# Decode attention with a gated MLP on one core: the last group of the output projection in four column tiles, as two parts in two banks

## The chip, the core and the metric

The kernel runs on one core of one Trainium2 chip. The metric is the device time of one execution in microseconds (us). Times of a kernel are medians of its executions. A profile is one further look at a single execution, and its span is some 2 us shorter than the time that the run reports.

Two short terms are used throughout. A **landing** is the moment at which the sixteenth of the sixteen DMA engines reports its share of a transfer; the trace keeps a record of each. The **tail** is the time from the last landing of the last group of `wo` (the very last load of the kernel) to the start of the final sum on VectorE.

## The reference

One decode step for 4 sequences: attention over a cache of 4096 keys for 32 heads of 128, its output projected by `wo`, plus a gated MLP, plus the residual. Only the projection matters here.

```python
o = jnp.einsum('bhqk,bhkd->bhqd', p, v_cache)
a = o.transpose(0, 2, 1, 3).reshape(B, Sq, H * Dh) @ wo      # [4, 4096] @ [4096, 640]
return x + a + mlp
```

## The kernel before

The heads are worked on in four groups of eight. For each group the attention output is transposed into `oT`, 128 rows by 8 columns `c` of 4 sequences, and `wo` for the group lies in SBUF as 128 rows by 8 columns `c` by 640. Each `c` needs two matmuls, one for each half (`hf`) of the 640 outputs, so a group takes 16 matmuls of 320 columns with only 4 rows of output each. A column tile is here one of four places for a matmul, told by the partition at which its output starts: 0, 32, 64 or 96. In the trace of this kernel, four matmuls with four different ones start within 10 ns (656.971 to 656.981 us), and the next four 0.22 to 0.27 us later.

The first three groups, the MLP and the residual are summed in one PSUM tile `proj`. They use all four column tiles: even `c` on partitions 0 and 32, odd `c` on 64 and 96.

```python
def emit_proj(g, cs=range(HG)):
    oT = state[("oT", g)]
    for c in cs:
        for hf in range(NH):
            r0 = 64 * (c % 2) + 32 * hf
            nc.tensor.matmul(proj[r0:r0 + B, 0:NO2], lhsT=oT[:, c, :],
                             rhs=wo_t[g][:, c, hf * NO2:(hf + 1) * NO2], start=False, ...)
```

The last group has an accumulator of its own, so that `proj` can be emptied meanwhile, and uses two column tiles only. Its weights come last of all loads, in four pieces.

```python
load_wo(NG - 1, (0, 4, 6, 7, 8))        # c 0..3, 4..5, 6, 7
# ... (cut)
o_1 = ppool.tile([64, NO2], F32, tag="p", name="o_1")
nc.vector.tensor_copy(out=o_1[:], in_=proj[0:64, 0:NO2])                                          # L530
nc.vector.tensor_tensor(out=o_1[:], in0=proj[64:128, 0:NO2], in1=o_1[:], op=ALU.add)              # L531
last = ps_l.tile([64, NO2], F32)
for c in range(HG):
    lhsT = oT[:].rearrange("p c b -> p (c b)") if c == 0 else oT[:, c, :]
    for hf in range(NH):
        nc.tensor.matmul(last[32 * hf:32 * hf + (32 if c == 0 else B), :], lhsT=lhsT,             # L538
                         rhs=wo_t[NG - 1][:, c, hf * NO2:(hf + 1) * NO2], start=(c == 0), stop=(c == HG - 1))
nc.vector.tensor_tensor(out=o_bf[:], in0=last[:], in1=o_1[:], op=ALU.add)                         # L542
nc.sync.dma_start(out=out_flat[:, 0:NO2], in_=o_bf[0:B, :])
nc.scalar.dma_start(out=out_flat[:, NO2:NOUT], in_=o_bf[32:32 + B, :])
```

The first matmul of a half is 32 columns wide so that all 32 rows which VectorE reads later hold something written.

## Time and profile before

| | before |
|---|---|
| time, median of the first 3 runs | 665.66 us (665.23 to 665.97) |
| span of the profiled run | 663.9 us |
| busy share of PE, VectorE, ScalarE | 45%, 54%, 12% |
| read from HBM | 282.25 MB, 425 GB/s over the span |
| last landing | 660.03 us |
| tail | 0.87 us |
| last landing to the end of the span | 3.84 us |

The page gives one busy share for each engine, but these are averages over 660 us, in which no engine is the bound and the transfers are. What the change can move is the last 5 us, and those must be read by themselves. The prediction does so, and shows the lines. One more line is useful beside them: the instructions of the last projection by line of code, with the shortest, median and longest duration in ns and the first and last start.

```profile
L538 PE MATMUL last<-kv,oT x16: 425/471/474, 658.5 to 660.3; 128*4 128x320 bf16 x14, 128*32 128x320 bf16 x2
```

The sixteen matmuls start from 658.5 to 660.3 in 8 rounds of two, and each is in flight 0.47 us: they overlap, so a duration is not what a round costs. The step from one round to the next is.

### The profile page before, as it was taken

The page shows a single profiled execution, that of the slowest core. Times are in us where ns is not written, and L with a number is a line of the kernel's source. Part 1 is how long each engine was busy: PE and PEld are TensorE (multiplying, and loading weights), DVE is VectorE, ACT ScalarE, POOL GpSimd, SP SyncE. Part 2 cuts the span into 40 slices and gives each one's busy share as a digit, 9 for nine tenths or more (in the row PEclk, how much of TensorE's full clock was granted, in tenths as well). Part 3 has the DMA queues.
Part 4 walks back from the last instruction along what each step waited for, and adds up shares of the span by engine and source line. Part 5 has one row for each costly group of instructions (what it writes and reads, how often), then busy time and mean ns, then how long its engine had stood idle before and what let it go on. Part 6 is the DMA issues. An engine that isn't in the chain of part 4 may idle for free.

```text
span 663.9 us, 5636 instructions
## 1 busy us (share of the span) xinstructions
PE 298.9 (45%) x2394; PEld 112.8 (17%) x2394; DVE 360.7 (54%) x331; ACT 77.8 (12%) x162; POOL 10.2 (2%) x35
## 2 busy tenths in 40 slices
PE   0624765266072556225446175542506254633245
PEld 0401211122021122101112022110202112211012
DVE  5248999656190849509164286745628084950002
ACT  0300000430100000530200000070100000062200
POOL 3000000000000000000000000000000000000000
PEclk9998778768576587677757676766958768777767
DMA  9999999999999999999999999999999999999995
GB/s 372 461 434 416 423 451 434 430 435 435 415 442 435 430 414 440 440 430 431 438 438 431 426 422 436 440 438 435 426 430 427 434 433 420 452 431 428 425 414 229
DMA packets 6901, 282.61 MB, mean 426 GB/s; under 512 B 808, under 2 KB 1084, under 8 KB 1468
## 3 DMA queue, kind: packets, MB, share of 16 engines
q1 hardware_dynamic: 6856, 282.25, 98.6%
q8 instruction: 18, 0.29, 0.2%
q14 instruction: 7, 0.06, 0.0%
q10 hardware_dynamic: 20, 0.01, 0.0%
HBM read 282.25 MB, written 0.01 MB: 425 GB/s over the span
## 4 chain that ended last, share of the span: by engine, by line
DMA 71%; issue 12%; DVE 12%; PE 3%; ACT 1%; DVEq 0%; SPq 0%; ACTq 0%
DMA kv<-in_A_k_cache_dram 61%; DVE kT L361 11%; DMA kv<-in_A_v_cache_dram 5%; DMA kv<-in_A_wo_dram 3%; DMA kv<-in_A_wq_dram 2%; PE O L443 2%; PE q L262 1%; PE S L372 0%; ACT xd L426 0%; ACT Zb L407 0%; PE last L538 0%; ACT p L415 0%; DVE pT L419 0%; DVE kv L271 0%; DVE m L379 0%
## 5 line engine op out<-in xcount | busy, mean ns | idle before, releaser
L361 DVE STREAM_TRANSPOSE kT<-kv 128x2048 f32<-128x2048 f32 x128 | 282.8, 2275 | 127.4 <-DMA kv<-in_A_k_cache_dram 125.7
L372 PE MATMUL S<-kT,QZ 128*32 128x512 bf16 x1024 | 190.2, 505 | 232.5 <-DVE kT L361 232.5
L372 PEld LDWEIGHTS <-QZ 128*32 128x32 bf16 x1024 | 61.0, 112 | 356.5 <-issue 337.6
L443 PE MATMUL O<-kv,Zb 128*32 128x512 bf16 x1024 | 75.9, 462 | 59.8 <-DMA kv<-in_A_v_cache_dram 32.8
L450 DVE TENSOR_SCALAR R<-O,Mk 128x128 f32<-128x128 f32 x16 | 5.6, 350 | 126.9 <-PE O L443 126.9
L407 ACT ACTIVATE Zb<-xd,MkE 32x256 bf16<-32x256 bf16 x116 | 52.9, 498 | 109.2 <-PE O L443 107.7
L415 ACT ACTIVATE p<-S,negmax 128x512 bf16<-128x512 f32 x8 | 5.4, 682 | 402.0 <-DVE negmax L393 402.0
L443 PEld LDWEIGHTS <-Zb 128*32 128x32 bf16 x1024 | 33.3, 114 | 101.7 <-issue 60.9
L460 PE MATMUL misc<-R,SelR 128*32 128x128 f32 x32 | 6.4, 281 | 26.0 <-DVE R L452 26.0
L452 DVE SCALAR_TENSOR_TENSOR R<-O,Mk,R 128x128 f32<-128x128 f32 x48 | 16.8, 351 | 1.7
L426 DVE COPY xd<-pT 32x256 bf16<-32x256 bf16 x44 | 16.1, 365 | 0.7
L426 ACT COPY xd<-pT 32x256 bf16<-32x256 bf16 x20 | 12.2, 612 | 5.6 <-DVE pT L419 5.2
L347 POOL COPY QZ<-qT 32x32 bf16<-32x32 bf16 x16 | 5.1, 317 | 418.6 <-PE S L372 400.2
L419 DVE STREAM_TRANSPOSE pT<-p 128x1024 bf16<-128x1024 bf16 x4 | 5.0, 1245 | 6.6 <-ACT p L415 6.6
L460 PEld LDWEIGHTS misc<-R,SelR 128*32 128x32 f32 x32 | 2.2, 107 | 33.5 <-DVE R L452 24.8
L379 DVE TENSOR_REDUCE m<-S 128x2 f32<-128x1024 f32 x4 | 4.9, 1224 | 5.5 <-PE S L372 5.5
L286 PE MATMUL misc<-xnT,kv 128*32 128x4 bf16 (+1 forms) x120 | 6.2, 188 | 0.7 <-DMA kv<-in_B_w_in_dram 0.7
L286 PEld LDWEIGHTS <-kv 128*32 128x32 bf16 (+1 forms) x120 | 6.1, 142 | 1.6 <-DMA kv<-in_B_w_in_dram 1.6
L431 PE MATMUL misc<-rowsum,SelPe 128*32 128x1 f32 x16 | 2.0, 197 | 9.3 <-ACT p L415 9.3
L262 PE MATMUL q<-kv,xnT 128*32 128x512 bf16 x40 | 4.5, 631 | 3.9 <-DMA kv<-in_A_wq_dram 3.9
L463 DVE SCALAR_TENSOR_TENSOR om<-misc,rinv,MkH 32x1024 bf16<-32x1024 f32 x4 | 5.1, 1271 | 2.0 <-PE misc L460 2.0
L384 PE MATMUL misc<-dg,ones_f 128*128 128x256 f32 x8 | 2.7, 416 | 7.5 <-DVE dg L381 7.5
(96 smaller groups left out, 63.6 us busy)
## 6 DMA issues: line engine op xcount, KB each, us to landing
kv<-in_A_k_cache_dram SPq DMA_DIRECT2D x8, 4096.0 KB
kv<-in_A_v_cache_dram SPq DMA_DIRECT2D x1, 6144.0 KB
kv<-in_A_wq_dram SPq DMA_DIRECT2D x1, 5120.0 KB
kv<-in_A_wo_dram SPq DMA_DIRECT2D x3, 1280.0 KB
kv<-in_B_w_in_dram SPq DMA_DIRECT2D x1, 2160.0 KB, 19.8
kv<-in_A_v_cache_dram SPq DMA_DIRECT2D x1, 2048.0 KB
kv<-in_B_w_out_dram SPq DMA_DIRECT2D x1, 800.0 KB
kv<-in_A_wo_dram SPq DMA_DIRECT2D x1, 640.0 KB, 22.5
```

The source lines that it names most:

```text
L262: nc.tensor.matmul(q4_ps[32 * j:32 * j + 32, hf * 512:hf * 512 + 512], lhsT=xnT[:, c, :], rhs=wq[:, c, n0:n0 + 512], start=(c == 0), stop= ...
L286: nc.tensor.matmul(zT_ps[:n, part, fc, :], lhsT=w, rhs=xnT[:, c, 0:B], start=(c == 0), stop=(c == DC - 1))
L347: nc.gpsimd.tensor_copy(out=QZ[r0:r0 + 32, :, :, :, 8 + 8 * hp], in_=qT[32 * g:32 * g + 32, NE * hp:NE * hp + NE].rearrange("p e a b -> p ...
L361: nc.vector.transpose(kT[:].rearrange("p (t r) -> p t r", r=32), kw)
L372: nc.tensor.matmul(S_ps[32 * q:32 * q + 32, e], lhsT=QZ[:, b, 2 * kh + w, e, w0:w0 + 32], rhs=kb[:, i, :, e, :, w], start=(b == 0 and k < ...
L407: nc.scalar.activation(out=dst, in_=src, func=ACT.Copy, scale=mk)
L415: nc.scalar.activation(out=p_bf[:, :, e, :], in_=S_ps[:, e], func=ACT.Exp, bias=negmax[:, e:e + 1], scale=scale, accum_out=rowsum[:, e:e + 1])
L426: op(out=xd[32 * hp:32 * hp + 32, :, q, :], in_=pT[32 * q:32 * q + 32, :, hp, :].rearrange("p t x -> p x t"))
L443: nc.tensor.matmul(O_ps[32 * q:32 * q + 32, :, :], lhsT=Zb[b % 2][:, w].rearrange("p h c -> p (h c)"), rhs=vv[:, w * 4 * Dh:(w + 1) * 4 * ...
L450: nc.vector.tensor_scalar(out=R, in0=O_ps[:, 0, :], scalar1=Mk4[:, 0:1], scalar2=None, op0=ALU.mult)
L452: nc.vector.scalar_tensor_tensor(out=R, in0=O_ps[:, c, :], scalar=Mk4[:, c:c + 1], in1=R, op0=ALU.mult, op1=ALU.add)
L460: nc.tensor.matmul(oh[:], lhsT=SelR[:, b].rearrange("p h b -> p (h b)"), rhs=state["R"][:, b, :], start=(b == 0), stop=(b == B - 1))
```

## The change

Its intent is to project the last group as fast as the groups before it, with four column tiles. Columns 1, 3 and 5 go to partitions 64 and 96 of a second PSUM bank, while 0, 2, 4, 6 and 7 stay in the first. The second part is complete after `c = 5` and is added to `o_1` while PE still works on 6 and 7; then one sum closes as before. The first matmul of the second part reads 32 columns of `oT` from column 1 on, so `oT` has a ninth column of zeros.

```diff
-        oT = small.tile([P, HG, B], BF16, tag="oT", bufs=3)
-        nc.vector.tensor_copy(out=oT[:], in_=oT_ps[:])
+        oT = small.tile([P, HG + 1, B], BF16, tag="oT", bufs=3)
+        nc.vector.tensor_copy(out=oT[:, 0:HG, :], in_=oT_ps[:])
+        if g == NG - 1:
+            nc.gpsimd.memset(oT[:, HG, :], 0.0)
...
-    last = ps_l.tile([64, NO2], F32)
+    last_a = ps_l.tile([64, NO2], F32)
+    last_b = misc_ps([P, NO2], F32)
+    last = [last_a, last_b[64:128]]
     oT = state[("oT", NG - 1)]
+    part = {1: 1, 3: 1, 5: 1}
+    seen = set()
     for c in range(HG):
-        lhsT = oT[:].rearrange("p c b -> p (c b)") if c == 0 else oT[:, c, :]
+        p = part.get(c, 0)
+        lhsT = oT[:, c, :] if p in seen else oT[:, c:c + HG, :].rearrange("p c b -> p (c b)")
+        nb = B if p in seen else 32
         for hf in range(NH):
-            nc.tensor.matmul(last[32 * hf:32 * hf + (32 if c == 0 else B), :], lhsT=lhsT,
-                             rhs=wo_t[NG - 1][:, c, hf * NO2:(hf + 1) * NO2], start=(c == 0), stop=(c == HG - 1))
+            nc.tensor.matmul(last[p][32 * hf:32 * hf + nb, :], lhsT=lhsT,
+                             rhs=wo_t[NG - 1][:, c, hf * NO2:(hf + 1) * NO2], start=p not in seen, stop=c in (5, HG - 1))
+        seen.add(p)
+        if c == 5:
+            nc.vector.tensor_tensor(out=o_1[:], in0=last[1], in1=o_1[:], op=ALU.add)
...
-    nc.vector.tensor_tensor(out=o_bf[:], in0=last[:], in1=o_1[:], op=ALU.add)
+    nc.vector.tensor_tensor(out=o_bf[:], in0=last[0][:], in1=o_1[:], op=ALU.add)
```

In the changed kernel the matmuls are L546, the merge is L550 and the final sum L553.

## The prediction

> **What bounds the kernel now.** I read the page first, for what the whole span hangs on.
>
> ```profile
> PEclk9998778768576587677757676766958768777767
> DMA  9999999999999999999999999999999999999995
> GB/s 372 461 434 416 423 451 434 430 435 435 415 442 435 430 414 440 440 430 431 438 438 431 426 422 436 440 438 435 426 430 427 434 433 420 452 431 428 425 414 229
> ...
> DMA 71%; issue 12%; DVE 12%; PE 3%; ACT 1%; DVEq 0%; SPq 0%; ACTq 0%
> ```
>
> The transfers are busy nine tenths or more in 39 of 40 slices, at about 430 GB/s; only the last slice falls off. The kernel is one long stream of cache, and work on an engine costs time only where it lies behind the last bytes. The change touches nothing that starts a transfer, so all it can move is the tail. So the second view is the chain of waits, cut to the last microseconds (start, length, what):
>
> ```profile
> 635.91 22.53 DMA kv<-in_A_wo_dram
> 658.45 0.04 issue
> 658.49 2.33 PE last L538 x16
> 660.82 0.04 DVEq L542
> 660.86 0.04 issue
> 660.90 0.48 DVE o_bf L542
> ```
>
> It seems to say that after 658.45 the last projection (L538) is the whole path: 2.33 us of matmuls, then one sum of 0.48 us. This is what the change attacks. But a merged chain hides waits inside a group, so I looked at the same stretch in the timeline and in windows (length, then busy time of PE, PEld, DVE, ACT, POOL, then granted clock, DMA share, GB/s):
>
> ```profile
> 656.97 1.24 PE L482 MATMUL proj<-kv,oT 128*4 128x320 bf16 x16 [1.09 <-DMA kv<-in_A_wo_dram]
> ...
> 658.49 2.32 PE L538 MATMUL last<-kv,oT 128*32 128x320 bf16 x16 [0.28 <-DMA kv<-in_A_wo_dram]
> ...
> 658.77 0.49 DVE L531 TENSOR_TENSOR o<-proj,o 64x320 f32<-64x320 f32 x1
> ```
>
> ```profile
> 656.97:658.21 1.24, 1.24 (x16) 0.53 (x16) 0.00 (x0) 0.00 (x0) 0.00 (x0) 0.50 0.32 121
> 658.49:659.30 0.81, 0.81 (x8) 0.47 (x9) 0.74 (x2) 0.00 (x0) 0.00 (x0) 0.50 0.09 35
> 659.30:660.03 0.73, 0.73 (x8) 0.40 (x6) 0.00 (x0) 0.00 (x0) 0.00 (x0) 0.50 0.02 7
> ```
>
> Two things are to be seen. The projection of the group before it (L482) has as many matmuls of the same width at the same clock of 0.50, and takes 1.24 us: it uses four column tiles, L538 only two. And transfers still run after 658.49, at 9% and then 2%. That is wo itself: its last group comes in four pieces, columns 0 to 3, 4 and 5, 6, and 7, and the matmuls of c = 0, 4, 6 and 7 each wait for one. The single records of the trace give what the merged rows do not. The sixteenth and last landing of the four pieces is at 658.45, 659.22, 659.64 and 660.03. The matmuls of c = 0 to 7 start at 658.49, 658.71, 658.98, 659.24, 659.51, 659.78, 660.04 and 660.31. So PE is late for its piece by 0.29 us at c = 4, 0.40 at c = 6, and only 0.28 at c = 7. The stream is right behind the projection as a second bound.
>
> **What the Trainium skill says.** "TensorE: Matmul & The Clock Gate", Part 1 (the HAM clock gate), gives N / 1.2 ns between matmuls at half clock: 267 ns for 320 columns. The trace agrees: 658.710 to 658.977 is 267 ns between pairs. Part 3 of that page (packing small matmuls, row/col tiling) says that tiles overlap, some 4 ns apart. The trace agrees: L482's first four start within 10 ns (656.971 to 656.981), and its quads too are 267 ns apart. "DMA: Bandwidth & Descriptors", in the section on why a DMA increments its semaphore by 16, says that only the full 16 means that the data is there. The trace agrees and shows its price: the sixteen increments of the last piece come from 654.33 to 660.03, the fifteenth at 659.25; one late engine sets the end. "PSUM — Partial Sum Buffer", Terms, calls it an error when TensorE and another engine use one bank and quadrant at once; that fits the second bank, which VectorE reads while PE still writes the first. No run here shows it.
>
> **The change part by part.**
> - PE: the same 16 matmuls in the same order of c. The columns 1, 3 and 5 go to partitions 64 to 127 of a second bank, beside 0, 2 and 4, and 6 and 7 follow in the first. So 8 rounds become 5: (0,1), (2,3), (4,5), 6, 7. By rounds alone that takes away 3 x 0.267 = 0.80 us.
> - Its waits are other: two on PE at c = 1, one for a small memset on GpSimd and one for an older write of the reused bank. GpSimd has nothing else left and the memset needs at most what stands before the cast of oT (ended at 656.11), over 2 us early; the other is older. I put both at 0.
> - VectorE gets one more sum after c = 5, with the shape of L531: 493 ns.
> - The memset of 128x4 and the larger tile: off the path.
>
> Now with landings, taking 0.04 us from landing to start (658.45 to 658.49; 656.93 to 656.97). Round (0,1) starts at 658.49; (2,3) at 658.71, the step that c = 0 to 1 had; (4,5) could start at 658.98 but its piece lands at 659.22, so 659.26; c = 6 could start at 659.53 but lands at 659.64, so 659.68; c = 7 could start at 659.95 but lands at 660.03, so 660.07. Before, it started at 660.31. The second half of c = 7 starts 0.02 later and takes 0.474, ending at 660.56 (before: 660.81). The last sum starts 0.094 after (the step of before, 660.807 to 660.901), at 660.66, and ends at 661.14 instead of 661.38. **0.24 us** is left of the 0.80.
>
> The extra sum: round (4,5) ends at 659.26 + 0.02 + 0.47 = 659.75; sum from 659.84 to 660.34. VectorE's earlier sum L531 ended at 659.27, the final one starts at 660.66: 0.3 us of slack, so the merge costs nothing. Behind the final sum, the issue of the two stores and their end take the same 2.49 us (661.38 to 663.87). So 665.66 - 0.24 = 665.42, in round numbers **665.4 us**, or 0.04%.
>
> **The rivals.**
> 1. All 0.80 us arrive: 664.9. For it: the chain of waits charges the whole stretch to PE. Against: the last piece lands at 660.03, and c = 7 cannot start before it. It needs a run in which all pieces land 0.5 us earlier against PE.
> 2. Nothing arrives: 665.7. If the last group ran at clock 1.00, pairs would be some 0.135 us apart (L482 at clock 1.00: quads at 654.014, 654.149, 654.284), so even two column tiles would finish c = 6 before 660.03 and c = 7 would wait for its piece before and after. Against: PE did 66 matmuls in the 15 us before 645.9 and little from 651.8 to 656.9; the clock had dropped to 0.50 by 656.9, and I expect that in most executions.
> 3. The merge becomes the wait: if the sum of c = 1, 3, 5 started 0.3 us late, the final sum would wait for VectorE, and a slip of its full 0.49 us would eat the gain: 665.6. Against: the slack above; it holds at full clock too, since both ends of it hang on landings (659.22 and 660.03).
> 4. A worse PE pattern (two banks written in turn, or PE's queue held by the new waits) that stretches rounds to 0.5 us: even then c = 7 starts at 660.3, where it does now: 665.7.
>
> **Range and chances.** All rivals lie between 664.9 and 665.7. The noise is as large: the three runs of before span 665.23 to 665.97, three times my gain, and a stream of 283 MB moves from run to run[...]. I chose 664.8 to 666.0: 0.6 to each side of 665.4. Two per cent is 13 us; the whole tail behind the first wait of L538 is 5.4 us, so faster by over 2% is impossible, and slower needs a disturbance of the stream, to which nothing in the change gives cause: 0.005 each.
>
> **What would show each step.** In the profile after: four column tiles should show as L546 taking about 2.1 us from its first start (2.32 before) but busy with gaps, waiting for wo at c = 4, 6 and 7, where before only c = 0 waited; the chain of waits should end with a transfer of wo that lands near 0.5 us before the last matmul ends, and few matmuls behind it. L550 should end some 0.3 us before L553 starts. From the last landing to the start of the final sum: 0.63 us, where before it was 0.87. I am wrong if L546 runs without gaps and is 0.8 us shorter (rival 1), if its clock is 1.00 (rival 2), if L553 starts right at the end of L550 (rival 3), or if the transfers themselves end at another time by more than 0.5 us, which would be run-to-run and not the change.

## The result, and the profile after

| | before | changed |
|---|---|---|
| median | 665.82 us (665.23 to 666.35, 4 runs) | 665.23 us (664.75 to 665.72, 4 runs) |
| ratio | | 0.9991, 95% interval 0.9974 to 1.0009 |
| last landing in the profile | 660.034 us | 660.165 us |
| tail | 0.867 us | 0.571 us |
| last landing to the end of the span | 3.84 us | 3.54 us |

A ratio here is the mean time of one kernel's fast runs over that of the other's of the same rounds, so it is not quite the ratio of the medians quoted. The medians differ by 0.59 us, but the interval holds 1: by whole times alone, no gain is shown. The profiles can say more, because they fix where the stream of loads ended. From the last landing on, the changed kernel is 0.30 us faster (3.84 to 3.54). No view shows a cause for the rest of the difference between the medians, and the end of the stream moves by more than that from run to run: the two profiles of the kernel before have their last landings at 660.03 and 659.47.

The chain of waits of the changed kernel (start, length, what):

```profile
636.71 22.64 DMA kv<-in_A_wo_dram
659.35 0.04 issue
659.39 0.43 PE last_a L546 x2
659.82 0.01 PE misc L546 x2
659.83 0.83 PE last_a L546 x4
660.65 0.04 DVEq L553
660.69 0.04 issue
660.74 0.48 DVE o_bf L553
```

Before, the chain left the transfers at 658.45 with 2.33 us of matmuls to go. Now it leaves them at 659.35, the landing of the piece with `c = 4` and 5, with 1.27 us to go (0.43 + 0.01 + 0.83). The path has moved from PE towards the stream. It has moved further than this view says, for the last four matmuls, `c = 6` and 7, look like one unbroken stretch here. The timeline of the same stretch gives it away in its rows of weight loads (`PEld`); brackets hold the idle time before a row:

```profile
659.39 0.43 PE L546 MATMUL last_a<-kv,oT 128*4 128x320 bf16 x2
659.39 0.09 PEld L546 LDWEIGHTS <-oT 128*4 128x4 bf16 x4 [0.45 <-issue]
...
659.81 0.83 PE L546 MATMUL last_a<-kv,oT 128*4 128x320 bf16 x4
659.81 0.08 PEld L546 LDWEIGHTS <-oT 128*4 128x4 bf16 x2 [0.33 <-issue]
659.88 0.49 DVE L550 TENSOR_TENSOR o<-misc,o 64x320 f32<-64x320 f32 x1 [0.53 <-PE misc L546]
660.21 0.08 PEld L546 LDWEIGHTS <-oT 128*4 128x4 bf16 x1 [0.32 <-issue]
660.74 0.48 DVE L553 TENSOR_TENSOR o_bf<-last_a,o 64x320 bf16<-64x320 f32 x1 [0.36 <-PE last_a L546]
```

The weight loads stop for 0.45, 0.33 and 0.32 us, before `c = 4`, 6 and 7. "issue" is the wrong word for these gaps. The pieces land at 659.35, 659.77 and 660.16 by the records of landings, and the matmuls of `c = 4`, 6 and 7 start at 659.39, 659.81 and 660.21: each 0.04 after its landing. The wait stands on the matmul, and the weight load behind it is held up with it. At `c = 6` and 7 the matmul rows show no gap because a matmul is in flight longer (0.43) than the time between the starts (0.42 and 0.40). The gaps in the weight loads tell where PE waits, but not how long the landing held it up: a second round can follow a round that waited by 0.22 us (658.59 to 658.81), so by estimate `c = 7` was held up by 0.18 us, not 0.32. The merge L550 ends at 660.37 and the final sum starts at 660.74, 0.36 us later. Not all of this is to spare: where the final sum had to wait for the merge (e2, below), it started 0.13 us after its end, so some 0.23 us are.

The windows of the changed kernel in the same columns as the prediction's (the second runs from the landing for `c = 4` to the last landing):

```profile
657.05:658.29 1.24, 1.24 (x16) 0.52 (x16) 0.00 (x0) 0.00 (x0) 0.00 (x0) 0.50 0.40 154
...
659.39:660.16 0.77, 0.77 (x6) 0.17 (x6) 0.28 (x1) 0.00 (x0) 0.00 (x0) 0.50 0.02 8
```

The clock granted is still 0.50, and PE loads weights in 0.17 of the 0.77 us, against 0.40 of 0.73 in the kernel before: it waits.

### The profile page after: what moved, and what is told of

It is laid out like the page before. It is cut to its first block, busy times and chain, and to the rows that moved or that the text cites. A ratio compares the mean times of both kernels' runs of the same rounds, so it can differ in the third digit from the quotient of the medians.

```text
span 663.7 us, 5640 instructions
## 1 busy us (share of the span) xinstructions
PE 296.9 (45%) x2394; PEld 111.8 (17%) x2394; DVE 360.2 (54%) x332; ACT 77.8 (12%) x162; POOL 10.3 (2%) x36
## 4 chain that ended last, share of the span: by engine, by line
DMA 74%; DVE 11%; issue 11%; PE 2%; ACT 1%; SPq 0%; DVEq 0%; ACTq 0%
DMA kv<-in_A_k_cache_dram 64%; DVE kT L361 11%; DMA kv<-in_A_v_cache_dram 5%; DMA kv<-in_A_wo_dram 3%; DMA kv<-in_A_wq_dram 2%; PE O L443 2%; ACT xd L426 0%; ACT Zb L407 0%; ACT p L415 0%; DVE pT L419 0%; PE last_a L546 0%; DVE m L379 0%; PE misc L384 0%; PE S L372 0%; SPq L166 0%
## 5 line engine op out<-in xcount | busy, mean ns | idle before, releaser
L443 PE MATMUL O<-kv,Zb 128*32 128x512 bf16 x1024 | 73.6, 451 | 60.5 <-DMA kv<-in_A_v_cache_dram 33.5
```

The lines of the kernel that those rows point to most:

```text
L443: nc.tensor.matmul(O_ps[32 * q:32 * q + 32, :, :], lhsT=Zb[b % 2][:, w].rearrange("p h c -> p (h c)"), rhs=vv[:, w * 4 * Dh:(w + 1) * 4 * ...
```

## The experiments

The theory, called L in the expectations: the last landing is the floor, and the change only takes away what PE lagged behind it. The rival P: the path was PE alone, and each round taken away is worth 0.267 us. The rival N: nothing changed, and two profiles differed by chance.

The results, in three calls that shared their runs of the kernel before (medians 665.28 with 9 runs, 665.29 with 11 and 665.39 with 7). "Clock" is the one granted while the last group was projected.

| run | median us | ratio, 95% interval | clock | tail us | last landing to end of span us |
|---|---|---|---|---|---|
| before, first profile | 665.82 | | 0.50 | 0.867 | 3.84 |
| e11_before_again | 665.57 | 1.0002, 0.9987 to 1.0017 | 0.50 | 0.872 | 3.85 |
| changed, first profile | 665.23 | 0.9991, 0.9974 to 1.0009 | 0.50 | 0.571 | 3.54 |
| e1_again | 665.22 | 0.9999, 0.9986 to 1.0011 | 0.50 | 0.570 | 3.54 |
| e2_seven_too | 664.92 | 0.9995, 0.9982 to 1.0007 | 0.50 | 0.729 | 3.71 |
| e8_one_column | 665.27 | 0.9996, 0.9984 to 1.0009 | 0.50 | 0.579 | 3.55 |
| e7_quarters | 665.61 | 0.9997, 0.9983 to 1.0011 | 0.50 from 658.60, 0.10 us after its start | 0.450 | 3.62 |
| e5_before_warm | 665.44 | 0.9994, 0.9982 to 1.0006 | 1.00 | 0.440 | 3.41 |
| e6_after_warm | 664.86 | 0.9987, 0.9974 to 1.0000 | 1.00 | 0.440 | 3.41 |

No whole time in this table is clear of 1, with four or five runs of each kernel. The tails are another matter: the two kernels that were profiled twice have tails that agree within 0.005 us, so differences of 0.1 us can be read from them. The other kernels were profiled once.

### e1_again and e11_before_again: the two kernels once more

No edit.

> The changed kernel once more, for the noise and a second profile. The tail is told as the time from the last landing of the last group of wo to the start of the final sum: 0.87 us in the profile before, 0.58 in the first profile of the changed kernel. Theory L (the last landing is the floor; the change only takes away what PE lagged behind it): tail 0.55 to 0.63 again, whole time 0.2 to 0.4 us below before, inside the scatter. Rival P (the path was PE alone, so each round of two matmuls taken away is worth 0.267 us): tail 0.3 us or more shorter and whole time 0.8 us below. Rival N (nothing changed, both profiles are chance): tail anywhere between 0.55 and 0.9.

> The kernel before, unchanged, for a second profile of it and for the scatter of a kernel against itself. Theory L: tail from the last landing to the final sum 0.82 to 0.92 us again (0.87 in the first profile), clock 0.50 in the last group, and a ratio of 1.000 within 0.002. If the tail is below 0.75, what the first two profiles showed was chance.

Tails of 0.570 and 0.872 us: both expectations of L are met, and N falls. The two profiles of the kernel before also show where the scatter is. Their spans are 663.87 and 663.32 us, their last landings 660.03 and 659.47, and what follows the last landing is 3.84 and 3.85: all of the difference is the stream. The last projection takes 2.33 us in the chain of waits of both. e1's whole time happened to fall level with before, in its own five rounds (0.9999).

### e8_one_column: one round fewer, not three

```diff
-    part = {1: 1, 3: 1, 5: 1}
+    part = {1: 1}
...
-                             ... start=p not in seen, stop=c in (5, HG - 1))
+                             ... start=p not in seen, stop=c in (1, HG - 1))
-        if c == 5:
+        if c == 1:
```

> Only column 1 goes to the second part: 7 rounds where the change has 5 and before has 8. Theory L: one round of 0.267 us is nearly all of the lag that PE had at c = 7 (0.28 us), so c = 7 starts within 0.05 us of its landing; without a gap its matmuls take 0.474, so tail 0.60 to 0.66 us: nine tenths of the gain of the change. Rival P: a third of the gain (one of three rounds), tail 0.77 us. Rival N: 0.87 or anywhere.

The tail is 0.579 us, a little below what L expected: nearly all of the gain (0.29 of 0.30 us) with one of the three rounds, where P as put here has a third of it. The timeline of this kernel:

```profile
659.48 0.61 PEld L546 LDWEIGHTS <-oT 128*4 128x4 bf16 x6 [0.19 <-issue]
...
660.29 0.08 PEld L546 LDWEIGHTS <-oT 128*4 128x4 bf16 x1 [0.20 <-issue]
660.83 0.48 DVE L553 TENSOR_TENSOR o_bf<-last_a,o 64x320 bf16<-64x320 f32 x1 [0.77 <-PE last_a L546]
```

The weight loads still stop for 0.20 us before `c = 7`, whose piece landed at 660.25 in this run and whose matmul started at 660.29. At PE's own step of 0.267 us after `c = 6` (659.97) it would have started at 660.23, so the landing held it up by only 0.06 us: one round is just enough. The other two rounds only make PE wait longer.

P falls in two steps. With the full 0.267 us for each round, three would give 0.80, and the changed kernel gave 0.30; this run alone could not refute that form, for one round at 0.267 gives a tail of 0.60 as well. The form in which each of the three gives a third of the gain falls here.

### e2_seven_too: a fourth round away, and the merge late

```diff
-    part = {1: 1, 3: 1, 5: 1}
+    part = {1: 1, 3: 1, 5: 1, 7: 1}
...
-        if c == 5:
-            nc.vector.tensor_tensor(out=o_1[:], in0=last[1], in1=o_1[:], op=ALU.add)
+        if c == 6:
+            nc.vector.tensor_tensor(out=o_1[:], in0=last[0][:], in1=o_1[:], op=ALU.add)
...
-    nc.vector.tensor_tensor(out=o_bf[:], in0=last[0][:], in1=o_1[:], op=ALU.add)
+    nc.vector.tensor_tensor(out=o_bf[:], in0=last[1], in1=o_1[:], op=ALU.add)
```

The last number of `stop` moved with it, from 5 to 6.

> Column 7 goes to the second part as well, so 4 rounds of matmuls where the change has 5; the first part is summed after c = 6 and the second closes. Theory L: the fourth round takes nothing away, for c = 7 waits for its landing; but the merge can only start when c = 6 is done, some 0.17 us after the landing of 7 and it takes 0.49, so the final sum waits for VectorE: tail 0.70 us, 0.12 longer than the change, still shorter than before, whole time 0.1 us above the change. Rival P: one round fewer, tail 0.2 shorter than that of the change. It also shows whether the slack that the prediction gave the merge (0.3 us) is real.

```profile
659.27 0.43 PE L546 MATMUL misc<-kv,oT 128*4 128x320 bf16 x2
...
659.34 0.48 DVE L550 TENSOR_TENSOR o<-last_a,o 64x320 f32<-64x320 f32 x1 [1.43 <-PE last_a L546]
659.96 0.49 DVE L553 TENSOR_TENSOR o_bf<-misc,o 64x320 bf16<-64x320 f32 x1
```

The tail is 0.729 us, 0.16 longer than e1's. The final sum has no idle time in brackets: it follows the merge, which ended at 659.82, and not PE, whose last matmuls ended at 659.70. Rival 3 of the prediction is thus a real hazard, and the change avoids it by leaving both 6 and 7 in the first part. The late merge was expected to cost 0.12 us over the change's tail and cost 0.16; the step from the end of the merge to the final sum is 0.13 us here, not the 0.04 that I had put in.

### e5_before_warm and e6_after_warm: the same at full clock

Eighteen matmuls whose results nobody reads are put into PE's empty stretches of the last 14 us, in the kernel before and in the changed one. They write to the accumulator of the last group before its first real matmul clears it. (`last` is `last_a` in e6.)

```diff
+    def warm(n, w, r):
+        for _ in range(n):
+            nc.tensor.matmul(last[0:w.shape[-1], :], lhsT=w, rhs=r, start=True, stop=True)
+
     emit_proj(NG - 3)
+    vl = unit(("v", NU - 1), 192, T)
+    warm(12, vl[:, 0:64], vl[:, 0:NO2])
     emit_sel(NG - 1)
     emit_proj(NG - 2, range(0, 4))
     emit_oT(NG - 1)
+    warm(6, state[("oT", NG - 1)][:, 0:HG, :].rearrange("p c b -> p (c b)"), vl[:, 0:NO2])
```

> The kernel before with 18 idle matmuls put in PE's empty stretches of the last 14 us, so that the clock granted may still be 1.00 when the last group is projected (0.50 in both profiles so far); result right. If the clock is 1.00 there, theory L: pairs are 0.135 us apart, PE is never late for a piece, c = 7 starts within 0.05 us of its landing and takes 0.30: tail 0.42 to 0.48 us, 0.4 below before and below the change, with two column tiles only. Rival P: tail 0.87 - 8 x 0.13, that is near 0, which the landing forbids. If the clock is still 0.50, the tail is 0.87 and the run tells nothing.

> The changed kernel with the same idle matmuls. If the clock is 1.00 in the last projection: theory L, tail 0.42 to 0.48 us, the same as e5 within 0.05, for both stand behind the same landing: the change is worth nothing at full clock. Rival P: 3 x 0.135 = 0.4 us shorter than e5. If the clock is still 0.50: tail 0.58 as in the change.

The windows, from the start of the last group to the last landing and from there to the end of its matmuls, of e5:

```profile
658.70:660.27 1.57, 1.43 (x14) 0.63 (x14) 0.63 (x2) 0.00 (x0) 0.00 (x0) 1.00 0.11 42
660.27:660.62 0.35, 0.30 (x2) 0.08 (x1) 0.00 (x0) 0.00 (x0) 0.00 (x0) 1.00 0.00 0
```

and of e6:

```profile
658.54:660.11 1.57, 1.06 (x14) 0.36 (x14) 0.76 (x2) 0.00 (x0) 0.00 (x0) 1.00 0.06 21
660.11:660.46 0.35, 0.30 (x2) 0.08 (x1) 0.08 (x1) 0.00 (x0) 0.00 (x0) 1.00 0.00 0
```

The clock granted is 1.00. The projection takes the same 1.57 + 0.35 us with two column tiles as with four; four only leave PE idle for longer before the last landing. The tails are 0.440 us in both. At full clock the change is worth nothing. The chain of waits now leaves the transfers at the last landing itself, with two matmuls to go, in e5 (660.27) as in e6 (660.11).

The kernel before with these idle matmuls (e5) thus has a shorter tail than the changed kernel, by 0.13 us, and e6 is no better than e5. By whole times neither is clear of the kernel before.

### e7_quarters: four column tiles without a second part

The output is cut into quarters of 160 columns instead of halves, for every projection: `NH = 4`, quarter `j` on partition `32 * j`. There is then no second part, no ninth column, and `o_1` is one copy. Four stores replace two.

```diff
-    NH = 2
+    NH = 4
...
-                r0 = 64 * (c % 2) + 32 * hf
+                r0 = 32 * hf
...
-    o_1 = ppool.tile([64, NO2], F32, tag="p", name="o_1")
-    nc.vector.tensor_copy(out=o_1[:], in_=proj[0:64, 0:NO2])
-    nc.vector.tensor_tensor(out=o_1[:], in0=proj[64:128, 0:NO2], in1=o_1[:], op=ALU.add)
-    last = ps_l.tile([64, NO2], F32)
+    o_1 = ppool.tile([P, NO2], F32, tag="p", name="o_1")
+    nc.vector.tensor_copy(out=o_1[:], in_=proj[:, 0:NO2])
+    last = ps_l.tile([P, NO2], F32)
...
-    nc.sync.dma_start(out=out_flat[:, 0:NO2], in_=o_bf[0:B, :])
-    nc.scalar.dma_start(out=out_flat[:, NO2:NOUT], in_=o_bf[32:32 + B, :])
+    for j in range(NH):
+        q = nc.sync if j % 2 == 0 else nc.scalar
+        q.dma_start(out=out_flat[:, j * NO2:(j + 1) * NO2], in_=o_bf[32 * j:32 * j + B, :])
```

(The diff is against the kernel before; the MLP's and the residual's projections are cut in the same way.)

> Another way to use four column tiles: every projection writes the output in quarters of 160 columns on partitions 0, 32, 64 and 96, so there is no second part, no merge and no padding column, the last round is 160 columns wide, the final sum is 128x160 instead of 64x320; the price is four stores, two on each queue. Theory L (only what lies behind the last landing counts): matmuls of c = 7 take about 0.29 us instead of 0.43 (133 ns fewer), tail 0.45 us; the final sum takes about 0.37 us instead of 0.48 (an estimate from the 0.35 us of the 128x128 sums); so the end of the final sum lies 0.82 us behind the last landing (1.06 with the change, 1.35 before); the second store of each queue gives back up to 0.3 us. Whole time 0 to 0.3 us below the change. Rival P: the same 5 rounds' worth of array time or less, no better than the change by more than its shorter sum. If the stores cost over 0.3 us it is no better than the change.

```profile
660.67 0.33 DVE L541 TENSOR_TENSOR o_bf<-last,o 128x160 bf16<-128x160 f32 x1 [2.60 <-PE last L537]
661.02 0.65 SPq L544 DMA_DIRECT2D out_dram<-o_bf  x2
661.02 0.62 ACTq L544 DMA_DIRECT2D out_dram<-o_bf  x2
```

The tail is 0.450 us, as expected, and the final sum takes 0.325 (I had estimated 0.37), so it ends 0.775 us after the last landing, 0.28 sooner than in the changed kernel (0.571 + 0.482 = 1.053). But each queue now issues two stores, in 0.65 and 0.62 us, where one took 0.31 and 0.28. From the last landing to the end of the span it is 3.62 us, 0.07 more than with the change (3.54). From the end of the final sum to the end of the span it is 2.84 us, against 2.49: the second store took back all of the 0.28 and a little more, which the expectation had allowed for.

### e3, e4, e9, e10: no landing to wait for

In these the last group is projected with the weights of the group before it, which land about 3 us sooner. The result is wrong.

```diff
-                             rhs=wo_t[NG - 1][:, c, hf * NO2:(hf + 1) * NO2], ...
+                             rhs=wo_t[NG - 2][:, c, hf * NO2:(hf + 1) * NO2], ...
```

e3 is the kernel before with this edit, e4 the changed kernel, e9 the kernel e8, and e10 is e4 without the merge L550. The comparison with the reference passed all four, wrong as they are. Presumably the projection of this group is too small a part of the output for it; no run shows why. So the comparison says nothing about these 16 matmuls in any kernel of this study; that the change computes the right thing rests on reading its diff.

> Wrong result on purpose. The kernel before, but the last group is projected with the weights of the group before it, which are there earlier, so that its matmuls wait for no landing of their own; the loads all stay. Counted from the last landing of that earlier group (656.93 in the profile before) to the start of the final sum: 3.97 us before. Theory L: the 8 rounds now follow the projection before them without a wait, first start about 1.06 us after the landing, 8 rounds at 0.267, end and hand over 0.59 after the last start: 3.5 us. Whole time 0.4 us below before.

> Wrong result on purpose. The changed kernel in the same way, 5 rounds and no landing to wait for. From the last landing of the earlier group to the start of the final sum, theory L: PE alone 3.5 - 0.80 = 2.7 us, but the merge stands behind the two sums that empty the other accumulator and then has no slack: 2.9 us, so 0.6 to 0.8 us shorter than e3, two to three times the 0.29 that the change gave with the landings in place. Whole time 0.6 us below e3. If the landing is not what cut the gain (rival: PE's rounds are simply not slower with two column tiles than with four, or the new waits cost what the rounds gave), e4 is only 0.3 us shorter than e3.

> Wrong weights on purpose, as e3 and e4: only column 1 in the second part, and no landing to wait for. 7 rounds. Theory L: start of c = 0 to start of c = 7 is 6 steps of 0.267, 1.60 us (1.87 in e3, 1.07 in e4); the merge comes right behind the sum L533 and has ended before PE has, so the final sum waits for PE: from the last landing of the earlier group to the final sum 0.27 us below e3 at the same clock, some 3.1 to 3.25 us, against 3.38 in e3 and 3.07 in e4. If a round taken away is worth less than 0.2 us even without landings, the theory is short of something.

> Wrong result on purpose. e4 without the merge: the second part is computed and never added. In e4 the merge stood behind L533 and the final sum behind the merge, and the final sum began 0.36 us later than PE's end alone would have let it. Theory: without the merge the final sum starts 0.09 to 0.10 us after the last matmul's end: from the landing of the earlier group 2.70 us if all of the stretch runs at clock 0.50, 2.57 if its first quad runs at 1.00; that is 0.37 below e4. Rival (the two waits or PE cost it): still 3.0 or more.

| | e3 | e4 | e9 | e10 |
|---|---|---|---|---|
| median us | 664.95 | 664.13 | 664.52 | 663.79 |
| ratio to before | 0.9986 | 0.9978 | 0.9987 | 0.9976 |
| clock while the last group was projected | 0.50 | 0.50 | 1.00, 0.50 from 657.30 | 1.00 |
| first to last round, start to start, us | 1.87 | 1.07 | 1.21 | 0.54 |
| landing of the earlier group to the final sum, us | 3.38 | 3.07 | 2.54 | 1.95 |

e3 and e4 give the worth of the three rounds when nothing lands in between: 1.87 - 1.07 = 0.80 us, exactly what the round count says. Yet the final sum came only 0.31 us sooner in e4, the value that I had written down for the rival, not the 0.6 to 0.8 of the theory. The profiles say why, and it is neither the landing nor what the rival named. In e3 the first quad (four matmuls) of the projection before still ran at clock 1.00, which gave e3 0.13 us (from the landing to its first matmul L538 it is 0.93 us, in e4 1.06 to the first L546; it is also why e3 came to 3.38 and not to the 3.5 expected). The other 0.36 us is VectorE. The end of e4's chain of waits:

```profile
656.38 1.26 PE proj L484 x16
...
657.66 0.49 DVE o L532
...
658.18 0.50 DVE o L533
...
658.78 0.50 DVE o L550
...
659.40 0.48 DVE o_bf L553
```

The last projection on PE is no longer in it. VectorE empties `proj`, adds its second half, merges, and closes, one behind the other. PE's last matmul ended at 658.94, and the final sum waited for the merge until 659.40; at PE's usual hand-over of 0.10 us it would have started at 659.04. So 0.80 - 0.13 - 0.36 = 0.31. At equal clock it would be 0.44 by this estimate: even with no landing to wait for, the change would not give all of its 0.80, for VectorE's sums are the next bound.

e9 and e10 were meant to take these apart at clock 0.50 and did not: the clock happened to fall later in these two profiles, at 657.30 and 658.36 (655.31 in e4, 656.57 in e3), so part or all of their last group ran at 1.00. Their times by PE cannot be held against e3 and e4, and my numbers for both are missed. What they do give is VectorE's own path, which did not change with PE's clock. From the start of the first copy to the start of the final sum it is 1.74 us in e4, 1.74 in e9 and 1.14 in e10: the merge costs 0.595 us wherever VectorE is the path, 0.492 of work and 0.103 of hand-over. In e10 the final sum even then waited for VectorE (L533 ended at 658.71, PE at 658.32).

## Why the prediction was right

**What bounds the kernel.** Right. The span follows the last landing: two profiles of one kernel differ by 0.55 us in span and 0.56 in landing (e11).

**Eight rounds become five, 0.80 us by rounds alone.** Right: 1.87 against 1.07 us (e3, e4).

**The landing leaves 0.24 of it.** The mechanism is right; the gain was under-estimated: it is 0.296 us (0.867 - 0.571) in the first pair of profiles and 0.302 in the second (0.872 - 0.570). The prediction had a tail of 0.63 us. The term that was mis-sized is the last round: I took 0.02 us to its second matmul and the 0.474 us of a matmul that queues behind others. After the wait its second matmul started 0.003 us after the first and took 0.425, so the round took 0.43 us, not 0.49. The start itself, 0.04 us after the landing, was right and gives 0.23 of the gain.

**The new waits on PE cost 0.** Right: the first matmul of `c = 1` started at 658.599, 0.006 us after that of `c = 0`.

**The merge costs nothing, with 0.3 us of slack.** Right: 0.36 counted in the same way, from end to start, of which some 0.23 could have been lost without cost. e2 shows what happens without the slack, and e4 that the slack exists only because PE is held by the landings.

**Rival 1, all 0.80 us.** Fell: `c = 7` starts 0.04 us after its landing in the changed kernel, and in e8 one round gave nearly all that three gave. **Rival 2, nothing at full clock.** Right about its effect (e5 and e6: 0.440 both) and right that it is not the usual case: in every profile here of a kernel with the right weights and no idle matmuls the clock had dropped to 0.50 by 658.60 us, at times from 655.32 on. **Rivals 3 and 4** did not occur in the change itself.

**The noise is as large as the gain.** Right. The median moved from 665.82 to 665.23, on my 665.4 within 0.2, but only about half of that difference is the change; e1 saw no difference at all in its medians (665.22 against 665.28). The gain of 0.3 us is shown by the profiles alone. So the agreement of the whole time is luck: the range 664.8 to 666.0 held every rival, and no whole time in it could have told them apart.

**What the views would show.** One point was wrong: the chain of waits does not end with the last landing. It names the landing of `c = 4` at 659.35 and then shows PE as unbroken, because matmuls in flight cover the waits. The gaps had to be read from the weight loads.

## What to carry to other kernels

When the last work stands behind a stream that comes in pieces, compare each piece's landing with the start of the work that needs it: the gain of faster work is about the lag at the last piece (0.28 us here, of which 0.04 stays) and what the very last step itself gets shorter (0.07), not the work saved (0.80). A chain of waits that shows a long stretch on one engine can hide waits inside it; look for idle time in the weight loads, and for starts that follow a landing by a constant 0.04 us. Once the last landing is the floor, only what comes after it counts (one matmul, its clock, the sum, the stores), and there a second store can cost as much as the rest gains. What no run here touched is larger: the first of the sixteen engines reports the last piece 4.1 to 5.9 us before the last one does (654.33 and 660.03 before), in every profile with the right weights.

## What the Trainium skill lacked or had wrong

- "TensorE: Matmul & The Clock Gate", Part 1, in its table of the two states, has the clock fall back to half after an idle window of about 3.4 us. Here it fell after a window in which PE was anything but idle: in the kernel before, from 652.75 to 656.15, PE was busy 1.78 of 3.40 us as the profile counts matmuls, and the clock was 0.50 from 656.16 on. In e6 it stayed at 1.00 after windows with 2.44 and 2.23 us of matmuls. And at half clock 2.32 us of 3.41 (656.16 to 659.57, before) did not raise it, while 3.35 did (645.92 to 649.33). These are no threshold: earlier in the kernel before, 1.55 us of 3.41 (581.07 to 584.48) kept the clock at 1.00, so the busy time that the profile counts does not decide it alone.
- The same page, under single matmul latency, gives (219 + N) / 1.2 ns at half clock, 449 ns for 320 columns and 316 for 160, for weights of 128 columns. Here the weights have 4 columns, so it is another case: a matmul that started after a wait took 422 to 428 ns (changed kernel) and 289 to 295 (e7); one that queued behind others 471 to 474. At full clock its (398 + N) / 2.4 gives 299, and 296 to 299 was measured (e5, e6).
- "DMA: Bandwidth & Descriptors", under latency and other measured facts, knows slower DMA engines and, as a best guess, lays them to rings that transfers issued from GpSimd use. No load here is issued from GpSimd, those of `wo` all from the Sync engine, and still one engine was mostly late with the last piece: the fifteenth report came at 659.25 and the sixteenth at 660.03 before, 659.56 and 660.165 in the changed kernel; in e8 two came together, at 660.24 and 660.25, 0.8 us after the fourteenth. Which engines they were, the records do not say.
- "Perfetto Trace Analysis", under identifying dependency chains, says that an instruction which waits on several engines may get a semaphore instruction ahead of it, and gives no cost. On VectorE the step from one sum to the next that depended on it was 0.03 us without one (L530 to L531, before) and 0.10 to 0.13 us with such an instruction between (e4: L533 to L550, L550 to L553).
